# Two scatters of token rows and three groups of transposing fetches, moved behind the recurrent loop

## The chip, the core and the metric

The kernel runs on one core of a Trainium2 chip. The core has five engines with queues of their own: PE (TensorE, matrix products; its weight loads are shown apart as PEld), DVE (VectorE), ACT (ScalarE), POOL (GpSimd) and SP (SyncE, which here only issues transfers). Transfers run on 16 DMA engines that all queues share. The metric is device time of one launch in microseconds (us), the median of several runs; lower is better.

## What is computed

Three stages follow each other: a gated linear recurrence over 768 positions for 4 x 8 heads, a layer of 8 experts of which each of the 3072 tokens takes its best two, and a dense layer with a tanh-like nonlinearity.

```python
# recurrence, t = 0..767
state = f[:, :, t, :, None] * state + np.einsum('bhd,bhe->bhde', k[:, :, t], v[:, :, t])
y[:, :, t] = np.einsum('bhd,bhde->bhe', q[:, :, t], state)
...
logits = x @ w_gate
noisy_logits = logits + log1p(exp(x @ w_noise)) * noise
top2 = argpartition(-noisy_logits, 2, axis=1)[:, :2]                # two experts for each token
for e in range(8):
    h = maximum(x[mask] @ w1[e], 0.0)
    out[mask] += top2_w[mask, k, None] * (h @ w2[e])
...
h = x @ w_in
g = h - tanh(h)
return g @ w_out
```

## The kernel before, in words

**The recurrent loop.** The 768 positions of 4 batches are cut into 24 blocks of 128, and a loop `for j in range(NT)` (NT = 24) takes one block in each iteration: scaled keys and queries (`scaled`, POOL's product at L468), scores (`scores`, L484), a mask on DVE (L490), outputs (`outputs`, L499 and L507), states, and the rows of x (`x_rows`, `x_split`). Iterations are counted from 0 in the code, so the 22nd and 23rd are j = 21 and j = 22.

**Routing and scatters.** Four blocks make a group. Three iterations after a group's last block, `place` works out the row in the table `xs` for each of its tokens and both of its experts. That makes 8 scatters for a group (4 blocks x 2 experts), 48 in all; here they are numbered 0 to 47. A scatter is an indirect DMA of 128 rows that POOL issues in `post` (L652). `post` is called twice in an iteration: once early, right behind the POOL product, and once behind `states`. The second call may be paced: POOL first copies one element of a result (`pace`, L327), so that it waits for that result. Early calls put a memset in front (L650) if the instruction before was a scatter as well. Behind the loop one scatter is posted in each step of the expert layer, paced by that step's activated tile `hs`. Table rows above 640 of each expert are cleared by 8 transfers (`clear`, L409) in the iterations j = 20 to 22.

**The expert layer.** `moe_steps` lists (expert, block, f): 8 steps f for each expert and block, the blocks in the order (0,0), (1,0), (2,0), (0,1), (1,1), and so on. Step n computes the first product of its own entry (`first_products`, L218, 9 matmuls that read all columns of the tile `xt`) and the second product of the entry two steps back (`second_products`, L237). Steps 0 to 2 lie in the loop's last iterations, 3 and 4 right behind it, the others in the loop over n. So n = 8 is the first step of (1,0), n = 16 that of (2,0), n = 24 that of (0,1).

**Fetches of expert parts.** `load_x(e, blk, pieces)` fills `xt` with transposing transfers from `xs` (L188), 128 rows to a piece, issued by SP. A fetch must come behind the scatters that can write its rows. For three blocks the code bounds those: `EARLY` says that (1,0) needs the blocks j < 16, that is scatters 0 to 31, and (2,0) needs j < 20, scatters 0 to 39. A later block, (0,1) too, needs all 48.

**What sets the order.** The schedule is written by hand: each engine runs its instructions in the order of the program. SP is one such queue: a fetch that waits for a scatter holds up all behind it, the expert weights (`load_weights`, L149, through a ring of 4 buffers, split on ACT and DVE at L158 and L159), the stores of results (L274) and the fetches of later weights (`decode_load`, L783).

Of the kernel before, what the change touches and what calls it, by code (L numbers as in the profile page):

```python
# [21 lines left out]
B, H, S, D = 4, 8, 768, 48  # L22
N, DM, NE, FF, F2 = 3072, 384, 8, 1024, 2048
NCH = S // 128
NT = B * NCH
# [5 lines left out]
def blocks(e):  # L31
    cut = {0: 320, 1: 384, NE - 1: 384}.get(e, 512)
    return (0, cut), (cut, CAP - cut)
# [3 lines left out]
EARLY = {(0, 0): 12, (1, 0): 16, (2, 0): 20}  # L37
# [40 lines left out]
def fast(ctx, tc, flag, f_cols, kq_cols, v_rows, gates, blank, void, w12, w_in, w_out, out):  # L78
# [96 lines left out]
    scatters = []  # L175
    xtp = ctx.enter_context(tc.tile_pool(name="xtp", bufs=3))

    def new_xt(key):
        XT[key] = xtp.tile([128, 6, 512], F16, name="xt")

    def load_x(e, blk, pieces):
        if pieces.start == 0:
            new_xt((e, blk))
        at, n = blocks(e)[blk]
        lo, hi = pieces.start * 128, min(n, pieces.stop * 128)
        if lo >= hi:
            return
        t = nc.sync.dma_start_transpose(XT[e, blk][:, :, lo:hi], xs[e * CAP + at + lo:e * CAP + at + hi, :])  # L188
        if (e, blk) in EARLY:
            early_rows[e, blk].append(t)  # L190
            for o in scatters[:2 * EARLY[e, blk]]:
                tc.add_manual_dep(t.ins, o.ins.name, mybir.DependencyInfo(mybir.DependencyClass.Sync, mybir.DependencyReason.DATA),
                                  reason="rows of earlier tokens")
            for o in scatters[2 * EARLY[e, blk]:]:
                tc.declare_no_dep(t.ins, o.ins, reason="slots of late tokens are clamped to later rows")
# [130 lines left out]
    def pace(t):  # L326
        nc.gpsimd.tensor_copy(spacer, t)  # L327
# [27 lines left out]
    with ExitStack() as actx:  # L355
# [3 lines left out]
        T = {}  # L359
# [199 lines left out]
        groups = [[4 * g + i for i in range(4)] for g in range(NT // 4)]  # L559
        ends = {js[-1] for js in groups}  # L560
        group_of = {j: g for g, js in enumerate(groups) for j in js}
# [82 lines left out]
        def post(n, behind=None):  # L644
            while n and posts:
                r, j = posts.pop(0)
                if behind is not None:
                    pace(behind)
                elif near[0]:
                    nc.gpsimd.memset(spacer, 0.0)  # L650
                near[0] = True
                sc = nc.gpsimd.indirect_dma_start(  # L652
                    out=xs, out_offset=bass.IndirectOffsetOnAxis(ap=yslot[:, j, r:r + 1], axis=0),
                    in_=T["x16", j], in_offset=None)
                for o in scatters:
                    tc.declare_no_dep(sc.ins, o.ins, reason="slots of other tokens")
                for o in clears if j < CLEARED else ():
                    tc.declare_no_dep(sc.ins, o.ins, reason="these tokens' slots lie below the cleared rows")
                for key, first in EARLY.items():
                    for o in early_rows[key] if j >= first else ():  # L660
                        tc.declare_no_dep(sc.ins, o.ins, reason="slots of late tokens are clamped to later rows")
                scatters.append(sc)
                n -= 1

        chains, posts = [], []
        LOGITS, ROWS, PLACES = ({js[-1] + i: g for g, js in enumerate(groups)} for i in (1, 2, 3))
# [36 lines left out]
        for j in range(NT):  # L703
            if j == NT - 4:
                load_v(NT - 1)
            else:
                load_all(j + 3)
            if j == NT - 5:
                load_kq(NT - 1)
                load_x(0, 0, range(3))  # L710
            for e in {NT - 4: (0, 1, 2), NT - 3: (3, 4, 5), NT - 2: (6, 7)}.get(j, ()):
                clear(e)
            if j == NT - 1:
                load_x(1, 0, range(1))
            scores(j + 1)
            carried(j)
            scaled(j + 2)
            post(1)
            decays(j + 2)
            mask(j + 1)  # L720
            copies = [step(at[j]) for step, at in ((group_logits, LOGITS), (group_rows, ROWS)) if j in at]
            for c in copies:
                next(c)
            if j in PLACES:
                advance(100)
                chains.append(place(PLACES[j]))
                advance(1)
            decay(j + 3)
            logs(j + 3)
            sums(j + 3)  # L730
            for c in copies:
                next(c, None)
            outputs(j)
            advance(2)
            states(j)
            post(j > min(PLACES), None if j // B < NCH - 1 else T["yT", group_of[j]][0:1, j - groups[group_of[j]][0], 0, 0:1])
            if j >= NT - 3:
                moe_first(*moe_steps[j - NT + 3])
            key_rows(j + 1)
            advance(2)  # L740
            if j:
                x_rows(j - 1)
                x_split(j - 1)
            weights(j)
            advance(2)
# [2 lines left out]
        tags.update(ph=cycle(("b3", "b6", "b4", "b7")))  # L748
        moe_first(*moe_steps[3])
        post(1, corner(((0, 0), 3)))  # L750
        load_x(1, 0, range(1, 2))
        last = len(groups) - 1
        for _ in group_logits(last):
            pass
# [9 lines left out]
        advance(100)  # L764
        moe_products(4)
        post(1, corner(((0, 0), 4)))
        load_x(1, 0, range(2, 3))

    gath = ctx.enter_context(tc.tile_pool(name="gath", bufs=4))
    win = ctx.enter_context(tc.tile_pool(name="win", bufs=1))  # L770
# [126 lines left out]
    for n in range(4, len(moe_steps) + LAG):  # L897
        if n > 4:
            moe_products(n)
        if n == 5:  # L900
            chains.append(place(last, "b3"))
            advance(100)
        if n >= len(moe_steps):
            put_results()
            continue
        e, blk, f = moe_steps[n]
        nxt = order[n // 8 + 1] if n // 8 + 1 < len(order) else None
        if n > 4:
            post(1, corner(((e, blk), f)))
        if n == 12:  # L910
            rows_of = count_rows()
        if n == 14:
            take_rows(rows_of)
        if 9 <= n < 13:
            assert len(scatters) >= 2 * EARLY[2, 0]
            load_x(2, 0, range(n - 9, n - 8))
        for _ in range(2 if n < 6 else 1):
            if ahead:
                split_weights(*ahead.pop(0))
                if coming:  # L920
                    load_weights(*coming.pop(0))
        if n == 20:
            nc.sync.dma_start(y_rows[(NE - 2) * CAP + 512:(NE - 1) * CAP, :], void)
        if n == 17:
            assert not posts
            nc.vector.tensor_tensor(dv, top2[:, :, 1], top2[:, :, 0], op=OP.subtract)
            nc.scalar.activation(wt[:, 1, :], dv, AF.Exp)
            nc.vector.tensor_scalar(wt[:, 0, :], wt[:, 1, :], 1.0, 1e-9, op0=OP.add, op1=OP.add)
            nc.vector.reciprocal(wt[:, 0, :], wt[:, 0, :])
            nc.vector.tensor_scalar(wt[:, 0, :], wt[:, 0, :], SM / (SX * SW * SW), None, op0=OP.mult)  # L930
            nc.vector.tensor_tensor(wt[:, 1, :], wt[:, 1, :], wt[:, 0, :], op=OP.mult)
        if nxt and 17 <= n < 21 or n >= 24 and f < 4 and nxt:
            assert not posts
            load_x(*nxt, range((n - 1) % 8, (n - 1) % 8 + 1) if n < 24 else range(f, f + 1))
        m = n - len(moe_steps) + 16
        if 3 <= m < 11:
            gather_y((m - 3) // 2, (m - 3) % 2, corner(((e, blk), f)))
        if m == 7:
            new_xt(("m", 0))
        if m in (6, 9, 11, 13):  # L940
            combine((m - 6) // 2)
        if m in (7, 10, 12, 14):
            put_m((m - 7) // 2)
        if e >= 2 and blk == (e in (2, NE - 1)):
            if f < 5:
                load_weights(e + 1, f + 3)
            split_weights(e + 1, f)
        if f >= 5:
            if 0 < e < NE - 2 and blk == 1:
                load_weights(e + 2, f - 5)  # L950
            if e == NE - 1 and blk == 0:
                load_weights(NE, f - 5)
        if e < NE - 1:
            for i in range(2) if e < 2 else (blk,):
                if blk or e >= 2:
                    weight_sum(e, f, i)
        for _ in range((2 if f == 2 else 1) if f in (2, 4, 6) else 0):
            if DEC:
                decode_put(*DEC.pop(0))
        if n > 12 and f % 2 and todo:  # L960
            if loads_ahead:
                decode_load(*loads_ahead.pop(0))
            decode_work(*todo.pop(0))
        if 9 < n < 13:
            decode_load(*loads_ahead.pop(0))
        put_results()
# [83 lines left out]
    for n in range(M + FF_LAG):  # L1050
        if n < M:
            blk, f = steps[n]
# [315 lines left out]
```

## Time and profile before

| what | value |
|---|---|
| median of 3 runs | 892.25 us (891.9 to 892.9) |
| the profiled execution | 893.01 us, span 891.2 us |
| PE busy | 879.7 us, 99% of the span |
| ACT, DVE, POOL busy | 67%, 64%, 20% |
| chain that ended last | PE 95%, POOL 1%, ACT 1%, DMA 1%, "issue" 1% |
| mean granted TensorE clock | 0.996 of full speed |
| DMA: SP's queue / POOL's queue | 40.5% / 7.1% of 16 engines' span |

How to read it: the span is what the profiler saw of the program on the core, and the execution's own time is a little longer. PE is busy nearly all the time, so a wait of PE makes the launch longer by its whole length, and work of another engine counts only where PE waits for it. The loop ends near 123 us; the steps n = 5 to n = 24 lie between 127 and 190 us.

### The profile page before, as it was taken

What the parts mean: (1) busy time and instruction counts of PE and PEld (TensorE: products, weight loads), DVE (VectorE), ACT (ScalarE), POOL (GpSimd) and SP (SyncE); (2) the same over time, 40 slices, a digit from 0 to 9 for tenths busy, and PEclk for the clock granted to TensorE, in tenths of its full rate; (3) what the DMA queues carried; (4) which work ended last, traced back from release to release, by engine and by line L of the source; (5) the groups of instructions that cost most, each with busy time, mean ns of one, the idle gap of its engine ahead of it and who ended that gap; (6) DMA issues with size and microseconds to landing.
All of it is one profiled execution on the core that took longest, in us unless ns stands there. A gap on an engine that the chain in (4) does not pass through costs nothing.

```text
span 891.2 us, 17622 instructions
## 1 busy us (share of the span) xinstructions
PE 879.7 (99%) x6380; PEld 528.4 (59%) x6380; DVE 574.7 (64%) x1167; ACT 599.8 (67%) x1561; POOL 175.5 (20%) x240
## 2 busy tenths in 40 slices
PE   9999999999999999999999999999999999999996
PEld 8888766555665656556566555555555555555553
DVE  8988965733486565667657766565565665665664
ACT  8989755656786566668658776666666567557653
POOL 3588835100000000000004050140230320410000
PEclk9999999999999999999999999999999999999999
DMA  9899898844595575739356523041230220320101
GB/s 271 199 260 285 271 296 253 274 104 82 163 245 172 145 216 110 213 105 240 105 152 170 148 67 44 19 101 24 61 74 10 72 63 10 90 53 1 37 1 40
DMA packets 112335, 116.86 MB, mean 131 GB/s; under 512 B 68208, under 2 KB 91376, under 8 KB 112080
## 3 DMA queue, kind: packets, MB, share of 16 engines
q1 hardware_dynamic: 105792, 96.11, 40.5%
q0 software_dynamic: 6144, 18.88, 7.1%
q8 instruction: 69, 1.13, 0.5%
q14 instruction: 42, 0.34, 0.1%
q10 hardware_dynamic: 288, 0.39, 0.1%
HBM read 72.88 MB, written 30.38 MB: 116 GB/s over the span
## 4 chain that ended last, share of the span: by engine, by line
PE 95%; POOL 1%; ACT 1%; issue 1%; DMA 1%; DVE 0%; SPq 0%; POOLq 0%
PE py L237 43%; PE ph L218 43%; PE pA L484 2%; PE pY L507 2%; PE pY L499 1%; PE warm L671 1%; DMA kq<-in_kq_cols 1%; PE pkr L523 1%; PE pX L550 1%; POOL kqT L468 1%; POOL xs L652 1%; PE pK L536 0%; PE pt L570 0%; ACT eneg L463 0%; ACT yT L513 0%
## 5 line engine op out<-in xcount | busy, mean ns | idle before, releaser
L237 PE MATMUL py<-wsplit,hs 128*128 128x384 f16 x2384 | 423.3, 326 | 0.0
L237 PEld LDWEIGHTS <-hs 128*128 128x128 f16 x2384 | 233.2, 98 | 164.8
L218 PE MATMUL ph<-xt,wsplit 128*128 128x512 f16 (+7 forms) x1152 | 213.2, 330 | 0.0
L218 PE MATMUL ph<-xt,winS 128*128 128x512 f16 x864 | 201.6, 379 | 0.0
L218 PEld LDWEIGHTS <-wsplit 128*128 128x128 f16 x1152 | 112.6, 98 | 78.2 <-issue 0.9
L862 DVE SCALAR_TENSOR_TENSOR s<-s,z 128x512 f32<-128x512 f32 x96 | 66.4, 692 | 137.2 <-ACT s L859 137.2
L858 ACT ACTIVATE z<-ph 128x512 f32<-128x512 f32 x96 | 57.3, 597 | 127.5 <-PE ph L218 127.5
L218 PEld LDWEIGHTS <-winS 128*128 128x128 f16 x864 | 84.5, 98 | 91.9
L252 DVE SCALAR_TENSOR_TENSOR hs<-ph,hs 128x256 f16<-128x256 f32 (+2 forms) x192 | 79.5, 442 | 80.9 <-ACT hs L244 80.2
L244 ACT ACTIVATE hs<-ph 128x512 f16<-128x512 f32 (+3 forms) x128 | 65.6, 513 | 81.0 <-PE ph L218 71.2
L159 DVE SCALAR_TENSOR_TENSOR wsplit<-raw,wsplit 128x768 f16<-128x768 f32 x72 | 68.6, 955 | 17.6 <-ACT wsplit L158 16.5
L164 ACT ACTIVATE junk<-wsplit 128x384 f16<-128x384 f16 x144 | 74.2, 515 | 1.4
L859 ACT ACTIVATE s<-z,bias_a 128x512 f32<-128x512 f32 x96 | 69.3, 722 | 3.1
L327 POOL CAST spacer<-hs 1x1 f32<-1x1 f16 x22 | 5.7, 258 | 329.1 <-ACT hs L244 328.5
L864 DVE SCALAR_TENSOR_TENSOR g<-s,ph 128x512 f32<-128x512 f32 x96 | 66.0, 687 | 6.1
L871 DVE TENSOR_TENSOR hs<-g,hs 128x512 f16<-128x512 f32 x96 | 65.7, 685 | 0.1
L158 ACT ACTIVATE wsplit<-raw 128x768 f16<-128x768 f32 x72 | 60.0, 834 | 3.9 <-DMA raw<-in_w 3.4
L327 POOL COPY spacer<-g 1x1 f32<-1x1 f32 x40 | 20.0, 500 | 215.9 <-DVE g L864 199.7
L870 ACT ACTIVATE hs<-g 128x512 f16<-128x512 f32 x96 | 58.8, 613 | 1.1 <-DVE g L864 1.1
L829 POOL DMA_INDIRECT g<-y_rows,yslot x48 | 52.8, 1099 | 19.6 <-issue 10.6
L652 POOL DMA_INDIRECT xs<-xkeep,yslot x48 | 49.7, 1035 | 15.9 <-issue 10.1
L266 ACT ACTIVATE yo<-py 128x384 f32<-128x384 f32 x26 | 12.7, 490 | 36.8 <-PE py L237 36.8
(149 smaller groups left out, 855.9 us busy)
## 6 DMA issues: line engine op xcount, KB each, us to landing
raw<-in_w SPq DMA_DIRECT2D x64, 384.0 KB
y_rows<-yo SPq DMA_DIRECT2D x48, 192.0 KB
kq<-in_kq_cols SPq DMA_DIRECT2D x42, 192.0 KB
w<-in_moe_w_out SPq DMA_DIRECT2D x32, 192.0 KB
w<-in_moe_w_in SPq DMA_DIRECT2D x24, 256.0 KB
v<-in_v_rows SPq DMA_DIRECT2D x24, 192.0 KB
out<-o SPq DMA_DIRECT2D x22, 192.0 KB
f<-in_f_cols SPq DMA_DIRECT2D x40, 96.0 KB
```

Source lines behind the costliest of these rows:

```text
L158: nc.scalar.activation(t[:, 0], raw, AF.Copy, scale=SW)
L159: nc.vector.scalar_tensor_tensor(t[:, 1], raw, SW, t[:, 0], op0=OP.mult, op1=OP.subtract)
L164: nc.scalar.activation(junk[:, :DM], RING[e, f][:, 0, 3 * i:3 * i + 3, :].rearrange("p a b -> p (a b)"), AF.Square, accum_out=wsum[:, 8 * ...
L218: nc.tensor.matmul(ph[:, :n], l, x[:, r, :n], start=(o == 0), stop=(o == 8))
L237: nc.tensor.matmul(p[:max(m, 128)], l, r, start=(f == 0 and o == 0), stop=(f == last and o == len(ops) - 1))
L244: nc.scalar.activation(hs[:, :n], ph[:, :n], AF.Relu, accum_out=hacc[:, at:at + 1])
L252: nc.vector.scalar_tensor_tensor(hs[:, at:at + hi - lo], ph[:, lo:hi], 0.0, hs[:, lo:hi], op0=OP.max, op1=OP.subtract)
L859: nc.scalar.activation(s, z, AF.Square, scale=1.0 / SZ, bias=bias_a)
L862: nc.vector.scalar_tensor_tensor(s, s, ZD, z, op0=OP.add, op1=OP.mult)
L864: nc.vector.scalar_tensor_tensor(g, s, 0.5, ph, op0=OP.mult, op1=OP.mult)
L870: nc.scalar.activation(hs[:, :512], g, AF.Copy)
L871: nc.vector.tensor_tensor(hs[:, 512:], g, hs[:, :512], op=OP.subtract)
```

## The change

The second `post` of the iterations j = 21 and j = 22 posts nothing any more. The scatters behind them move up by two places: the loop ends with scatter 31 in place of 33, and the last one, 47, is posted at n = 18 in place of n = 16. So that each fetch still stands behind the scatters that it needs, the fetches move too:

- (1,0): its three pieces were issued at j = 23, behind step 3 and behind step 4; now behind step 3, behind step 4 and at n = 5.
- (2,0): its four pieces were issued at n = 9 to 12, now at n = 11 to 14.
- (0,1): its four pieces were issued at n = 17 to 20, now at n = 19 to 22; the six small instructions that make the weights `wt` of the two experts move from n = 17 to n = 19.

```diff
@@ -181,6 +181,7 @@
     def load_x(e, blk, pieces):
         if pieces.start == 0:
             new_xt((e, blk))
+        assert (e, blk) not in EARLY or len(scatters) >= 2 * EARLY[e, blk], (e, blk, len(scatters))
@@ -710,8 +711,6 @@
-            if j == NT - 1:
-                load_x(1, 0, range(1))
             scores(j + 1)
@@ -733,7 +732,7 @@
             states(j)
-            post(j > min(PLACES), None if j // B < NCH - 1 else T["yT", group_of[j]][0:1, j - groups[group_of[j]][0], 0, 0:1])
+            post(j > min(PLACES) and j not in (NT - 3, NT - 2), None if j // B < NCH - 1 else T["yT", group_of[j]][0:1, j - groups[group_of[j]][0], 0, 0:1])
@@ -748,7 +747,7 @@
         post(1, corner(((0, 0), 3)))
-        load_x(1, 0, range(1, 2))
+        load_x(1, 0, range(1))
@@ -764,7 +763,7 @@
         post(1, corner(((0, 0), 4)))
-        load_x(1, 0, range(2, 3))
+        load_x(1, 0, range(1, 2))
@@ -911,9 +910,11 @@
-        if 9 <= n < 13:
+        if n == 5:
+            load_x(1, 0, range(2, 3))
+        if 11 <= n < 15:
             assert len(scatters) >= 2 * EARLY[2, 0]
-            load_x(2, 0, range(n - 9, n - 8))
+            load_x(2, 0, range(n - 11, n - 10))
@@ -921,7 +922,7 @@
-        if n == 17:
+        if n == 19:
             assert not posts
             nc.vector.tensor_tensor(dv, top2[:, :, 1], top2[:, :, 0], op=OP.subtract)
@@ -929,9 +930,9 @@
-        if nxt and 17 <= n < 21 or n >= 24 and f < 4 and nxt:
+        if nxt and 19 <= n < 23 or n >= 24 and f < 4 and nxt:
             assert not posts
-            load_x(*nxt, range((n - 1) % 8, (n - 1) % 8 + 1) if n < 24 else range(f, f + 1))
+            load_x(*nxt, range(n - 19, n - 18) if n < 24 else range(f, f + 1))
```

**POOL's queue at the end of the loop, before**, from the last product for the loop (L468) on. L652 is a scatter out of a group's rows (`xkeep0`: group 3, `xkeep1`: group 4), L474 a copy of decays, L327 the pacing copy, L650 the memset:

```order
L468 TENSOR_TENSOR kqT_2072<-eneg_2069,kq2_152 128x512
L652 DMA xs_61<-xkeep0_174,yslot_96 6656x768
L474 COPY gall_95<-eneg_2069 128x4
L327 COPY spacer_94<-yT_2033 1x1
L652 DMA xs_61<-xkeep0_174,yslot_96 6656x768
L650 MEMSET spacer_94 1x1
L652 DMA xs_61<-xkeep0_174,yslot_96 6656x768
L327 COPY spacer_94<-yT_2033 1x1
L652 DMA xs_61<-xkeep0_174,yslot_96 6656x768
L650 MEMSET spacer_94 1x1
L652 DMA xs_61<-xkeep1_175,yslot_96 6656x768
```

The same place now (line numbers are one higher):

```order
L469 TENSOR_TENSOR kqT_2072<-eneg_2069,kq2_152 128x512
L653 DMA xs_61<-xkeep0_174,yslot_96 6656x768
L475 COPY gall_95<-eneg_2069 128x4
L653 DMA xs_61<-xkeep0_174,yslot_96 6656x768
L651 MEMSET spacer_94 1x1
L653 DMA xs_61<-xkeep0_174,yslot_96 6656x768
L328 COPY spacer_94<-yT_2033 1x1
L653 DMA xs_61<-xkeep0_174,yslot_96 6656x768
L328 CAST spacer_94<-hs_2267 1x1
L653 DMA xs_61<-xkeep1_175,yslot_96 6656x768
```

Behind the copy of decays two scatters still follow each other with no wait for another engine's result; the third of that row, scatter 31, now belongs to j = 23. The first scatter of group 4 has moved behind the loop and waits for an `hs` tile first.

**SP's queue around the fetch of (2,0), before** (`xt_2572` is the tile of (2,0); `raw` are expert weights, `w64` later weights, `y_rows` results; DMASW in the brackets are the scatters' semaphores):

```order
L188 DMA_TRANSPOSE xt_2572<-xs_61 128x6x128 [waits DMASW5_49,DMASW4_49,DMASW6_49,DMASW3_49,DMASW7_49,DMASW2_49,DMAHW6_49,DMASW1_49,DMASW0_49]
L149 DMA raw_2577<-in_w12 128x768 [waits DMAHW2_49,DVE_49]
L274 DMA y_rows_62<-yo_2560 128x384 [waits Activation_49,Pool_49]
L274 DMA y_rows_62<-yo_2562 128x384 [waits DVE_49]
L274 DMA y_rows_62<-yo_2564 64x384 [waits DVE_49]
L188 DMA_TRANSPOSE xt_2572<-xs_61 128x6x128 [waits DMAHW3_49]
L149 DMA raw_2613<-in_w12 128x768 [waits DMAHW4_49,DVE_49]
L783 DMA w64_2615<-in_moe2_w_out 128x192 [waits DMAHW5_49,PE_49,Pool_49]
L188 DMA_TRANSPOSE xt_2572<-xs_61 128x6x128 [waits DMAHW6_49]
L149 DMA raw_2646<-in_w12 128x768 [waits DMAHW7_49,DVE_49]
L783 DMA w64_2648<-in_moe2_w_out 128x192 [waits DMAHW0_49]
L188 DMA_TRANSPOSE xt_2572<-xs_61 128x6x128 [waits DMAHW1_49]
```

The same fetch now (its tile is `xt_2634`):

```order
L275 DMA y_rows_62<-yo_2559 64x384 [waits DVE_49]
L149 DMA raw_2605<-in_w12 128x768 [waits DMAHW3_49,DVE_49]
L782 DMA w64_2607<-in_moe2_w_out 128x192 [waits PE_49,Pool_49]
L189 DMA_TRANSPOSE xt_2634<-xs_61 128x6x128 [waits DMASW5_49,DMASW4_49,DMASW6_49,DMASW3_49,DMASW7_49,DMASW2_49,DMAHW4_49,DMASW1_49,DMASW0_49]
L149 DMA raw_2639<-in_w12 128x768 [waits DMAHW5_49,DVE_49]
L782 DMA w64_2641<-in_moe2_w_out 128x192 [waits DMAHW6_49]
L189 DMA_TRANSPOSE xt_2634<-xs_61 128x6x128 [waits DMAHW7_49]
L149 DMA raw_2680<-in_w12 128x768 [waits DMAHW0_49,DVE_49]
L782 DMA w64_2682<-in_moe2_w_out 128x192 [waits DMAHW1_49]
L189 DMA_TRANSPOSE xt_2634<-xs_61 128x6x128 [waits DMAHW2_49]
L149 DMA raw_2713<-in_w12 128x768 [waits DMAHW3_49,DVE_49]
L782 DMA w64_2715<-in_moe2_w_out 128x192 [waits DMAHW4_49]
```

The stores of results and two weight loads now stand ahead of the first piece; between two pieces there is always one load of expert weights and one of later weights. The fourth piece is the next row behind those shown.

## Rows read from the trace of the kernel before

**Rows 1.** The page, part 1: busy time of each engine.

```profile
PE 879.7 (99%) x6380; PEld 528.4 (59%) x6380; DVE 574.7 (64%) x1167; ACT 599.8 (67%) x1561; POOL 175.5 (20%) x240
```

**Rows 2.** Chain that ended last, 85 to 175 us: start, duration, what.

```profile
109.95 0.54 issue
...
111.02 1.18 issue
...
113.49 2.51 PE ph L218 x9
...
118.22 1.33 PE ph L218 x9
```

**Rows 3.** Windows of 2 us: length, five engines' busy time, clock, DMA share, GB/s.

```profile
110.00:112.00 2.00, 0.53 (x3) 0.28 (x3) 1.18 (x3) 0.00 (x0) 0.98 (x2) 1.00 1.03 417
112.00:114.00 2.00, 1.80 (x17) 1.20 (x17) 1.11 (x4) 0.47 (x1) 0.00 (x0) 0.71 1.00 417
114.00:116.00 2.00, 2.00 (x9) 1.27 (x8) 0.00 (x0) 0.13 (x1) 1.22 (x3) 0.50 0.97 390
```

**Rows 4.** Timeline of POOL, the scatters: start, duration, what, idle before.

```profile
108.92 0.99 POOL L652 DMA_INDIRECT xs<-xkeep,yslot  x1 [0.16 <-issue]
...
110.22 0.97 POOL L652 DMA_INDIRECT xs<-xkeep,yslot  x1 [0.21 <-issue]
...
114.95 0.97 POOL L652 DMA_INDIRECT xs<-xkeep,yslot  x1 [0.52 <-DMA xs<-in_blank]
...
122.47 0.98 POOL L652 DMA_INDIRECT xs<-xkeep,yslot  x1 [0.16 <-ACT junk L247]
...
139.00 1.75 POOL L652 DMA_INDIRECT xs<-xkeep,yslot  x1 [0.51 <-issue]
...
145.95 0.98 POOL L652 DMA_INDIRECT xs<-xkeep,yslot  x1 [0.16 <-issue]
...
162.81 0.98 POOL L652 DMA_INDIRECT xs<-xkeep,yslot  x1 [0.51 <-issue]
```

**Rows 5.** Timeline of PE: start, duration, what.

```profile
135.88 1.63 PE L218 MATMUL ph<-xt,wsplit 128*128 128x384 f16 x9
...
159.11 2.10 PE L218 MATMUL ph<-xt,wsplit 128*128 128x512 f16 x9
...
162.51 2.10 PE L218 MATMUL ph<-xt,wsplit 128*128 128x512 f16 x9
...
189.27 1.87 PE L218 MATMUL ph<-xt,wsplit 128*128 128x448 f16 x9
```

**Rows 6.** Timeline of SP's queue: start and time of issuing.

```profile
126.14 1.21 SPq L188 DMA_TRANSPOSE xt<-xs  x1
...
129.70 0.33 SPq L149 DMA_DIRECT2D raw<-in_w  x1
...
142.74 1.95 SPq L188 DMA_TRANSPOSE xt<-xs  x1
...
145.41 1.44 SPq L274 DMA_DIRECT2D y_rows<-yo  x3
...
151.46 0.42 SPq L783 DMA_DIRECT2D w<-in_moe_w_out  x1
151.94 2.15 SPq L188 DMA_TRANSPOSE xt<-xs  x1
...
167.82 1.21 SPq L188 DMA_TRANSPOSE xt<-xs  x1
...
176.19 1.30 SPq L188 DMA_TRANSPOSE xt<-xs  x1
```

**Rows 7.** DMA packets in three windows: 145 to 145.5, 157 to 157.5, 157.5 to 158.

```profile
DMA packets 274, 0.06 MB, mean 124 GB/s; under 512 B 274, under 2 KB 274, under 8 KB 274
...
DMA packets 325, 0.21 MB, mean 420 GB/s; under 512 B 294, under 2 KB 294, under 8 KB 325
...
DMA packets 79, 0.20 MB, mean 390 GB/s; under 512 B 16, under 2 KB 16, under 8 KB 79
```

## The prediction, as it went on record

> **What bounds the kernel now.** I read the page first. PE is busy for 879.7 us of a span of 891.2 [rows 1], so whatever the other engines do counts only where PE stops. So next the chain of waits: it shows where PE stops, and it has long pieces of PE alone from 113 us to the end. The only stop near the change is in iteration j = 22: two pieces called "issue", 0.54 and 1.18 us, in which PE waits for nothing that the profile shows [rows 2]. The windows show what follows: PE works 0.53 us out of the 2 us from 110 on, and then the granted clock is 0.71 and 0.50 of full speed for two windows, the lower of the chip's two levels (1.2 instead of 2.4 GHz) for much of that time [rows 3]. The same nine matmuls that take 1.33 us at full clock take 2.51 there [rows 2]. Then I looked at where PE will need the fetched tiles, in PE's timeline: n = 8 starts at 135.88, n = 16 at 159.11, n = 24 at 189.27 [rows 5]. SP's timeline says when the pieces are issued [rows 6], and the packet counts when they land: a piece moves in packets under 512 bytes, and nothing else here does so in such number [rows 7].
>
> About 0.2% (1.8 us) is what a measurement of this kernel can tell from no change.
>
> **The change part by part.** The sum is made against the profiled execution's own 893.01 us; the median of the runs is 892.25, 0.76 lower.
>
> *The two scatters out of j = 21 and j = 22.* By name the change takes a scatter (0.99 us of POOL) out of each. But POOL's last product for the loop stands ahead of both, so nothing that PE waits for gets earlier. And the order shows what takes their place: the scatters of the next early calls move up. Before, scatters 29 and 30 started at 108.92 and 110.22 and scatter 31 at 114.95 [rows 4]. Now 29 and 30 still follow directly behind the same copy, so until 114.95 POOL and the DMA queues carry the same load, and PE's stop at 110 to 112 lies before that. I take 0 for it. Only scatter 31 leaves that stretch, 128 rows of 1536 bytes or 0.2 MB out of a stream of about 400 GB/s [rows 3], 0.5 us of DMA time that PE does not wait for. The ends are a gain of 3.1 us, if the stop goes with its slow clock (a rival below), and a loss of 0.5.
>
> *The pieces of (1,0), needed at n = 8.* SP no longer stops for scatter 31 inside j = 23. What is late next is scatter 31 itself, posted in the second place of j = 23, which before started at 122.47 [rows 4]. The third piece used to be issued at 126.14; it now stands behind the load that was issued at 129.70 [rows 6], so it starts near 130.05. With the slowest landing that the trace has (5.56 us, below) it is there at 135.6, and n = 8 starts at 135.88: 0.3 us to spare. I take 0, at most 1 us.
>
> *The pieces of (2,0), needed at n = 16.* This is the term. All nine matmuls of n = 16 read all four pieces.
> - The first piece waits for scatter 39. Before, this scatter started at 139.00, took POOL 1.75, and SP issued the piece at 142.74, 1.99 us behind its end [rows 4, 6]. Now scatter 39 takes the place that 41 had, in step n = 10: start 145.95, 0.98 us [rows 4]. The first piece is then issued at 145.95 + 0.98 + 1.99 = 148.92, 6.2 us later than before.
> - From the first piece's issue to the fourth's it was 151.94 - 142.74 = 9.20 us [rows 6]. SP was issuing without a pause, so what stands between counts: the three stores (1.44) are now ahead of the first piece, and one more load of later weights (0.42) stands between. 9.20 - 1.44 + 0.42 = 8.18, so the fourth piece is issued at 157.10.
> - How long a piece takes to land: the fourth, issued at 151.94, has its last large batch of small packets (294) before 157.5, and 16 in the next window: 5.56 us [rows 6, 7]. The first, issued at 142.74 into empty queues, is done by 145.5: 2.76 us [rows 6, 7]. Those are the two ends: 159.86 and 162.66. The nearer case is the slow one, since weight loads, later weights and scatters are queued between the pieces as before. I take off what the stores' 480 KB (by their shapes) cost there (1.2 us at 390 to 420 GB/s [rows 3, 7]) and add 0.5 for the additional load of 192 KB: 4.86 us, landing at 161.96.
> - PE would start n = 16 at 159.11. It stops for 161.96 - 159.11 = 2.85 us; the ends are 0.75 and 3.55. Nothing covers this: the second product of the same step stands behind the first in PE's queue.
> - The slow clock after it: the stop in j = 22 was shorter (0.54 + 1.18 us and little work between), and the clock fell behind it. The clock that was missing is 0.29 x 2 + 0.50 x 2 = 1.58 us [rows 3]; the nine matmuls alone lost 1.18 [rows 2]. I take 1.4; the ends are 0, if dense work ahead of the stop keeps the clock up, and 1.6.
>
> *The pieces of (0,1), needed at n = 24.* They wait for scatter 47, which moves by two steps of 162.51 - 159.11 = 3.40 us [rows 5], from 162.81 [rows 4] to 169.6. The first piece was issued 5.01 us behind that scatter's start, the fourth 8.37 behind the first [rows 6]: 174.6 and 183.0. With the slow landing it is there at 188.6, before 189.27; if PE stops at n = 16, both sides shift alike. 0, at most 1 us. The small instructions for `wt` move with SP's and DVE's slack; PE does not read them here. 0.
>
> The sum: 2.8 + 1.4 = 4.2 us. 893.01 + 4.2 = 897.2 for a profiled execution, and 896.4 as a median. The ends of the terms give +0.7 and +5.1, that is 892.9 to 897.4.
>
> **The rivals.**
>
> *A: the fourth piece of (2,0) is late* (above): 896.4.
>
> *B: it is in time.* SP no longer stands still before 142.74, so the loads and stores behind that wait go out earlier and the queues may be empty when the pieces come. Then a piece lands as the first one did, in 2.76 us, and everything turns on whether the fourth is issued before 159.11 - 2.76 = 156.35; I have 157.10. For it: 0.75 us is little, and the lost time of scatter 39 (1.75 before) may come back on POOL. Against it: SP needs some 8 us for the row of issues however empty the queues are, and between two pieces more transfers are queued than the DMA engines carry in that time. It gives 892.25, give or take 0.5. The Trainium skill ("DMA: Bandwidth & Descriptors", section "Anatomy of one DMA — SWDGE (gpsimd) path") speaks for it: it fits a fixed 2.0 us and the bytes at 436 GB/s, by which I estimate 2.45 us for a piece of 197 KB, a landing at 159.55 and a stop of only 0.4 us. The trace agrees for the first piece (2.76) and differs by a factor of two for the fourth (5.56), where other transfers are ahead of it.
>
> *C: faster, because PE's stop in j = 22 goes.* All engines are quiet from 110 to 112 while the DMA share is 1.03 and 1.00 [rows 3]; if traffic is what starves them, less of it helps. It would give back 0.54 + 1.18 and the 1.4 of slow clock, 3.1 us: 889.1, if the fourth piece is in time as well. It decides from the moment that scatter 29 or 30 starts later than now. Against it: by the order they do not.
>
> *D: a second tile is late too*, at n = 8 or n = 24, where I have 0.3 and 0.7 us to spare: about 1.5 us and once more 1.4 for the clock, on top of A: 899.3.
>
> **How the numbers follow.** A has 0.66, B 0.18, C 0.06, D 0.10. A is slower by more than 0.2% unless both its stop is near its lower end and the clock stays up: 0.58 slower, 0.08 within. B lies within 0.2% but for 0.01 that is faster. So faster 0.07, within 0.2% 0.25, slower 0.68. The predicted time is A's. The range 892.0 to 898.4 takes in A and most of B and leaves out C, a little of B below and the upper part of D.
>
> **What would show each step.** In the profile after: scatters 29 and 30 start within 0.5 us of 108.8 and 110, and the chain still has its "issue" and its slow clock at 110 to 116 (else C). The first piece of (2,0) is issued near 148.9 and the fourth near 157.1. PE's first matmuls of n = 16 have idle time before them, released by the fetch into `xt`, some 2.8 us long, and the next windows have a granted clock under 1. n = 8 and n = 24 start with no idle time. From n = 16 on, all of PE's work is later by one and the same amount. The prediction is wrong if PE goes through n = 16 without a stop, or if it stops where I have none.

## The result, and the profile after

The changed kernel takes 897.3 us (median of 6 runs, 896.28 to 899.16), the kernel before 892.58 in the same rounds (6 runs, 891.6 to 894.53). The ratio is 1.0053, with a 95% interval of 1.0037 to 1.0068: slower by 4.7 us. The prediction said 896.4, in a range of 892.0 to 898.4, and gave "slower" 0.68. The profiled execution took 897.11 us with a span of 895.3, against 893.01 and 891.2 before.

The page's part 1 after, which answers to [rows 1]:

```profile
span 895.3 us, 17624 instructions
...
PE 879.6 (98%) x6380; PEld 527.0 (59%) x6380; DVE 575.3 (64%) x1167; ACT 598.9 (67%) x1561; POOL 175.6 (20%) x239
```

PE has as many instructions and as much work as before; the span is 4.1 us longer. So PE stands still for longer. The waits of PE, summed over the whole span (line waited for, total us, times, longest), say where:

```profile
PE ph L219 <- issue: 3.6, 2, 3.3
```

One stop of 3.3 us, in front of a `ph` matmul. PE's timeline from n = 15 to n = 17 (start, duration, what, idle before it), to be held against [rows 5]:

```profile
155.11 1.63 PE L219 MATMUL ph<-xt,wsplit 128*128 128x384 f16 x9
156.57 1.63 PE L238 MATMUL py<-wsplit,hs 128*128 128x384 f16 x9
161.49 3.54 PE L219 MATMUL ph<-xt,wsplit 128*128 128x512 f16 x9 [3.30 <-issue]
164.83 1.92 PE L238 MATMUL py<-wsplit,hs 128*128 128x384 f16 x9
166.58 2.11 PE L219 MATMUL ph<-xt,wsplit 128*128 128x512 f16 x9
...
134.81 1.63 PE L219 MATMUL ph<-xt,wsplit 128*128 128x384 f16 x9
...
193.34 1.87 PE L219 MATMUL ph<-xt,wsplit 128*128 128x448 f16 x9
```

The third row is n = 16. PE was through with n = 15 and would have started at 156.57 + 1.63 = 158.20; it starts at 161.49. Then its nine matmuls take 3.54 us in place of 2.10, and the nine of the second product 1.92 in place of 1.63. The last two rows, n = 8 (with n = 7 ahead of it) and n = 24, have no idle time. The view names no releaser ("issue"). SP's queue (start, time of issuing) and the packets (windows 160 to 160.5, 160.5 to 161, 161 to 161.5) name it:

```profile
148.45 1.23 SPq L189 DMA_TRANSPOSE xt<-xs  x1
149.77 0.52 SPq L149 DMA_DIRECT2D raw<-in_w  x1
150.35 0.42 SPq L782 DMA_DIRECT2D w<-in_moe_w_out  x1
150.83 1.22 SPq L189 DMA_TRANSPOSE xt<-xs  x1
...
153.24 1.34 SPq L189 DMA_TRANSPOSE xt<-xs  x1
...
155.72 1.21 SPq L189 DMA_TRANSPOSE xt<-xs  x1
```

```profile
DMA packets 520, 0.14 MB, mean 276 GB/s; under 512 B 518, under 2 KB 518, under 8 KB 520
...
DMA packets 244, 0.18 MB, mean 362 GB/s; under 512 B 199, under 2 KB 199, under 8 KB 244
...
DMA packets 51, 0.16 MB, mean 313 GB/s; under 512 B 0, under 2 KB 0, under 8 KB 51
```

The small packets of the fetch end before 161; half a microsecond later PE runs. The fourth piece was issued at 155.72, so its packets are through after 5.3 us and PE starts after 5.77.

The windows of 2 us (length, busy time of PE, PEld, DVE, ACT and POOL, granted clock, DMA share, GB/s), at the end of the loop, which answers to [rows 3], and at the stop:

```profile
110.00:112.00 2.00, 1.04 (x28) 0.72 (x21) 1.58 (x4) 0.01 (x1) 1.78 (x3) 1.00 1.11 455
112.00:114.00 2.00, 1.69 (x19) 1.09 (x19) 1.77 (x4) 0.17 (x1) 0.26 (x1) 1.00 1.11 445
114.00:116.00 2.00, 2.00 (x29) 1.48 (x26) 0.21 (x1) 1.27 (x5) 0.00 (x0) 1.00 0.84 336
...
158.00:160.00 2.00, 0.20 (x2) 0.00 (x0) 1.30 (x3) 0.90 (x2) 0.98 (x1) 1.00 1.01 352
160.00:162.00 2.00, 0.51 (x3) 0.30 (x4) 0.91 (x3) 0.00 (x0) 0.00 (x0) 1.00 1.13 321
162.00:164.00 2.00, 2.00 (x7) 0.63 (x6) 0.00 (x0) 0.00 (x0) 0.00 (x0) 0.50 1.05 413
164.00:166.00 2.00, 2.00 (x9) 0.93 (x8) 0.16 (x1) 0.88 (x3) 0.06 (x1) 0.65 0.79 299
```

Behind the stop the granted clock is 0.50 and 0.65: the lower of the two levels, 1.2 GHz, for all of one window and most of the next. At the end of the loop PE still stops, but in this execution the clock stays at 1.00 there, where it had fallen to 0.71 and 0.50 before.

The balance, up to the start of n = 17 (166.58 against 162.51 [rows 5], 4.07 later): n = 16 was due 0.91 earlier than before (158.20 against 159.11); the stop adds 3.30, the first product's slow clock 1.44, the second's 0.29. That is 4.12, 0.05 more than the 4.07 because a product starts a little before the one ahead of it ends; the span is 4.1 longer. Nothing behind n = 17 adds to it: n = 24 is 4.07 later too (193.34 against 189.27 [rows 5]).

### The profile page after: what moved, and what is told of

Its sections match the earlier page's. It is cut to its first block, busy times and chain, and to the rows that moved or that the text cites. A ratio compares the mean times of both kernels' runs of the same rounds, so it can differ in the third digit from the quotient of the medians.

```text
span 895.3 us, 17624 instructions
## 1 busy us (share of the span) xinstructions
PE 879.6 (98%) x6380; PEld 527.0 (59%) x6380; DVE 575.3 (64%) x1167; ACT 598.9 (67%) x1561; POOL 175.6 (20%) x239
## 4 chain that ended last, share of the span: by engine, by line
PE 88%; POOL 6%; issue 2%; ACT 2%; DVE 1%; DMA 1%; POOLq 0%; DVEq 0%
PE py L238 43%; PE ph L219 42%; POOL xs L653 3%; POOL kqT L469 2%; PE pY L508 1%; POOL st L545 1%; DMA w<-in_moe_w_out 1%; PE pA L485 1%; POOL gall L475 0%; PE pY L500 0%; DMA f<-in_f_cols 0%; PE pkr L524 0%; ACT eneg L464 0%; PE pX L551 0%; ACT krows L526 0%
## 5 line engine op out<-in xcount | busy, mean ns | idle before, releaser
L653 POOL DMA_INDIRECT xs<-xkeep,yslot x48 | 51.6, 1075 | 12.6 <-issue 11.4
```

What stands on the lines that cost most here:

```text
L653: sc = nc.gpsimd.indirect_dma_start(out=xs, out_offset=bass.IndirectOffsetOnAxis(ap=yslot[:, j, r:r + 1], axis=0), in_=T["x16", j], in_off ...
```

## The experiments

The theory: the whole loss is the fourth piece of (2,0), late at n = 16, with the slow clock behind the stop. The rivals: that the scatters moved behind the loop, or the later fetch of (0,1), cost something themselves; and that the eight clears at the end of the loop feed PE's stop in j = 22. The first four share one set of runs of the kernel before (median 892.17 of 29), the last three another (892.39 of 28).

**The fetches back in their places, with the scatters of the changed kernel.** Two scatters each at n = 5 and 6 make up for the two that were left out (the comments in this diff and the next are added here, and lines are cut at `...`):

```diff
-            post(1, corner(((e, blk), f)))
+            post(2 if n < 7 else 1, corner(((e, blk), f)))
-        if 11 <= n < 15:
+        if 9 <= n < 13:                  # the pieces of (2,0)
-        if nxt and 19 <= n < 23 or ...
+        if nxt and 17 <= n < 21 or ...   # the pieces of (0,1), wt at 17
```

> The changed kernel, but two scatters are posted in each of the steps n = 5 and n = 6, so that scatter 39 is back at n = 8; the fetches of (2,0) and (0,1) stand at n = 9 to 12 and n = 17 to 20 again. The loop's end and the fetch of (1,0) stay as changed. Theory (the fourth piece of (2,0) is late, because scatter 39 gates the first): no stop at n = 16, some 5 us less than the changed kernel, 892 us or a little under, since the loop's end was 0.9 us shorter in the changed kernel's trace. Rival (moving scatters from the loop to the expert steps costs time by itself, by more DMA traffic there): between 894 and 897, with waits spread over n = 5 to 16.

Measured: 892.28 us, ratio to before 1.0008 [0.9996, 1.0021]. PE's timeline at n = 8 and at n = 16:

```profile
135.08 1.62 PE L219 MATMUL ph<-xt,wsplit 128*128 128x384 f16 x9 [0.33 <-DMA xt<-xs]
...
158.79 2.10 PE L219 MATMUL ph<-xt,wsplit 128*128 128x512 f16 x9 [0.33 <-DMA xt<-xs]
160.73 1.63 PE L238 MATMUL py<-wsplit,hs 128*128 128x384 f16 x9
```

The loss is gone although the loop's scatters are those of the changed kernel, and what is left of the stop at n = 16, 0.33 us, is now put down to the fetch into `xt`: PE starts 6.85 us behind the fourth piece's issue (151.94). The scatters outside the loop cost nothing that can be told from noise; the later fetches do. At n = 8, PE waits 0.33 us for the pieces of (1,0), which are fetched as in the changed kernel.

**The later fetches alone, with the scatters of the kernel before.**

```diff
-        if 9 <= n < 13:
+        if 11 <= n < 15:                 # the pieces of (2,0)
-        if nxt and 17 <= n < 21 or ...
+        if nxt and 19 <= n < 23 or ...   # the pieces of (0,1), wt at 19
```

> The kernel before with its scatters as they were, but the fetches of (2,0) and (0,1) two steps later in SP's program, as in the change. Theory (it is the scatter that the first piece waits for, not the place in the program): scatter 39 has landed long before, SP runs ahead of the steps, the first piece is issued near 145.3 and the fourth near 152.6, PE does not stop at n = 16: 892 to 893. Rival (the later place alone makes the fourth piece late): a stop of 2 to 3.5 us at n = 16 and 895 to 897.

Measured: 892.3 us, 1.0007 [0.9995, 1.0018]. PE's timeline:

```profile
157.36 2.10 PE L218 MATMUL ph<-xt,wsplit 128*128 128x512 f16 x9 [1.25 <-DMA w<-in_moe_w_out]
159.30 1.63 PE L237 MATMUL py<-wsplit,hs 128*128 128x384 f16 x9
```

I had expected no stop. There is one of 1.25 us: the first piece is issued at 143.28 and the fourth at 151.23, and PE starts 6.13 us behind that. PE itself is 3 us earlier here than in the kernel before (n = 15 starts at 153.03 against 156.18), so what counts is how far the fourth issue is ahead of n = 15: 1.80 us, against 4.24 before [rows 6]. In the kernel before with its clears spread (the last experiments), where n = 15 is early as well (154.47), it is 3.99 and there is no stop. So the later place in the program is enough for a stop, and the scatter that comes later makes it longer. The clock stays up behind 1.25 us. In the median the stop doesn't show, but the interval (up to 1.6 us) doesn't exclude it, and this profile has hardly a stop in j = 22 (PE is busy 1.71 of the 2 us from 110 on, at a clock of 1.00).

**The changed kernel with the four pieces of (2,0) back to back.**

```diff
-        if 11 <= n < 15:
+        if n == 11:
-            load_x(2, 0, range(n - 11, n - 10))
+            for i in range(4):
+                load_x(2, 0, range(i, i + 1))
```

> The changed kernel, but all four pieces of (2,0) are issued one behind the other at n = 11, with no weight loads between. The scatters stay as changed, so the first piece is still issued near 148.5. Theory (beside the gate, the two loads between each pair of pieces make the fourth late): the fourth is issued near 152.4 and lands by 157, no stop at n = 16, 892 us. Rival (the transposing fetches are slow by themselves and queue behind each other): the fourth lands after 159, a stop of 1 us or more, 894 or above.

Measured: 891.67 us, 0.9995 [0.9984, 1.0006]. SP's queue, then PE's timeline:

```profile
148.37 5.27 SPq L189 DMA_TRANSPOSE xt<-xs  x4
153.74 0.52 SPq L149 DMA_DIRECT2D raw<-in_w  x1
154.31 0.44 SPq L782 DMA_DIRECT2D w<-in_moe_w_out  x1
```

```profile
156.26 1.63 PE L238 MATMUL py<-wsplit,hs 128*128 128x384 f16 x9
157.73 2.10 PE L219 MATMUL ph<-xt,wsplit 128*128 128x512 f16 x9
```

The first piece waits for the same late scatter as in the changed kernel (148.37 against 148.45), yet n = 16 starts with no idle time: the fourth piece is issued some 3 us earlier, and no load is queued ahead of it. This also answers what the `w` in the stop of the run before is: the loads of later weights now go out behind the pieces, later than in the changed kernel, and PE doesn't wait for them. With one edit the whole loss is gone, so everything else that the change moves ((1,0), (0,1), `wt`, the two scatters) costs nothing that can be measured. It is the fastest version that was run, but it can't be told from the kernel before.

**The stop filled with work.** The changed kernel with 50 matmuls of 128 columns ahead of n = 16's first product, so that PE works while it waits:

```diff
+                if (e, blk, f) == (2, 0, 0):
+                    for _ in range(50):
+                        nc.tensor.matmul(ph[:, :128], ones, ones, start=True, stop=True)
```

> The changed kernel with 50 matmuls of 128 columns on a constant tile in front of the first product of n = 16, into the same bank, some 2.8 us at full clock, so that PE works while it waits; their sums are overwritten. Theory (of the 5 us, 3.3 are the stop and 1.7 the slow clock behind it): the first real matmul of n = 16 still starts near 161.5, the granted clock stays 1.00, the nine matmuls take 2.1 instead of 3.5 us: 1.5 to 1.8 us less than the changed kernel, near 895.6. Rival (the nine matmuls are slow for another reason, such as reading a tile that is still being written): no gain, 897.3 or more.

Measured: 895.73 us, 1.0037 [1.0023, 1.0051], 1.6 us less than the changed kernel's median (1.4 by the two ratios). PE's timeline and its windows:

```profile
156.27 1.63 PE L219 MATMUL ph<-xt,wsplit 128*128 128x384 f16 x9
...
159.20 2.96 PE L297 MATMUL ph<-ones 128*128 128x128 bf16 x50
163.09 2.10 PE L219 MATMUL ph<-xt,wsplit 128*128 128x512 f16 x9 [0.94 <-issue]
165.03 1.63 PE L238 MATMUL py<-wsplit,hs 128*128 128x384 f16 x9
```

```profile
160.00:162.00 2.00, 2.00 (x39) 1.98 (x36) 1.83 (x5) 0.07 (x1) 0.36 (x1) 1.00 1.15 272
162.00:164.00 2.00, 1.06 (x8) 0.46 (x6) 0.21 (x1) 0.00 (x0) 0.00 (x0) 1.00 1.12 355
...
110.00:112.00 2.00, 0.81 (x17) 0.44 (x9) 1.32 (x3) 0.00 (x0) 0.97 (x1) 1.00 0.92 383
112.00:114.00 2.00, 1.94 (x24) 1.51 (x25) 1.77 (x4) 0.60 (x1) 0.00 (x0) 0.87 1.11 451
114.00:116.00 2.00, 2.00 (x10) 1.39 (x9) 0.00 (x0) 0.30 (x1) 0.00 (x0) 0.50 0.95 390
```

n = 16 comes no earlier (6.82 us behind n = 15's start, 6.38 in the changed kernel), but at full clock: 2.10 and 1.63. So the two parts of the loss are apart: 1.73 us in the rows (3.54 and 1.92 in the changed kernel) are the clock, the rest is the wait. The medians agree (1.6 us) but don't show it by themselves, since the intervals of the two ratios overlap. The last three rows are from the end of the loop of the same execution: there the clock did fall this time, with the same instructions as in the changed kernel, so this execution (897.15 us) is no faster than the changed kernel's profile. Its mean granted clock is 0.996; four of the six executions have 0.997 to 0.999, while all six of the changed kernel have 0.995 or 0.996.

**Half of the change.** One scatter fewer (in j = 22 alone), the fetches one step later:

```diff
-            post(j > min(PLACES) and j not in (NT - 3, NT - 2), ...
+            post(j > min(PLACES) and j != NT - 2, ...
-        if 11 <= n < 15:
+        if 10 <= n < 14:
-        if nxt and 19 <= n < 23 or ...
+        if nxt and 18 <= n < 22 or ...
```

> Half of the change: only j = 22 posts one scatter fewer, so the last scatters move by one place; the fetches of (2,0) and (0,1) move by one step (n = 10 to 13 and n = 18 to 21), that of (1,0) as in the change. Theory (the fourth piece follows scatter 39, one step of some 2.9 us for each place; the changed kernel's stop was 3.3 us, the time to spare before about 1.5): the fourth piece comes some 2.9 us earlier than in the changed kernel, the stop at n = 16 is 0.3 to 0.6 us and too short for the clock to fall: 892 to 893. Rival (the stop does not follow the scatter's place, but comes from the queues being full at that time): a stop of 1.5 us or more, 894 to 896.

Measured: 894.54 us, 1.0023 [1.0005, 1.0041]. SP's queue, then PE's timeline:

```profile
146.02 1.22 SPq L189 DMA_TRANSPOSE xt<-xs  x1
...
153.21 2.00 SPq L189 DMA_TRANSPOSE xt<-xs  x1
```

```profile
159.31 2.10 PE L219 MATMUL ph<-xt,wsplit 128*128 128x512 f16 x9 [1.25 <-DMA w<-in_moe_w_out]
161.25 1.63 PE L238 MATMUL py<-wsplit,hs 128*128 128x384 f16 x9
```

The pieces go out 2.4 to 2.5 us earlier and the stop is 2.05 us shorter, without the slow clock in this execution: the stop falls with the lateness, as the theory wants. The stop is larger than I had expected (1.25 us): PE starts 6.10 us behind the fourth piece's issue. My figure for the landing was too short again. The median is above the theory's 892 to 893, in the rival's range, though the stop is not the 1.5 us that the rival wanted. The profiled execution (893.28 us, mean granted clock 0.999) is among the faster of the eleven; four have 0.992 to 0.995 and take 894.02 to 900.75 us. So this version loses its clock in some executions; where, no trace shows.

**The eight clears spread over j = 15 to 22**, in the kernel before and in the version with the pieces back to back:

```diff
-            for e in {NT - 4: (0, 1, 2), NT - 3: (3, 4, 5), NT - 2: (6, 7)}.get(j, ()):
+            for e in range(max(0, j - NT + 9), j - NT + 10) if NT - 9 <= j < NT - 1 else ():
```

> The kernel before, its 8 clearing transfers spread over the iterations j = 15 to 22, one in each, in place of eight within j = 20 to 22. It asks where PE's stop with no named wait at 110 to 112 us comes from, which varies from run to run. Theory (that stop comes from the DMA queues being full of clearing transfers): PE goes through j = 22 without it and without the slow clock behind it in the profile, 889 to 891, and the runs lie closer together. Rival (it has another cause, or the spread transfers hold up the loads of earlier iterations by as much): 892 or more, with the idle time still there or moved to j = 15 to 20.

> The changed kernel with the four pieces of (2,0) issued together at n = 11 and the clearing transfers spread over j = 15 to 22. Theory (both stops have their own cause and add up): no stop at n = 16, none in j = 22, as fast as the kernel before with the spread alone or up to 0.5 us faster, 889 to 891. Rival (the spread gives nothing): 891.5 to 892.5, as with the pieces together alone.

Measured: 892.97, 1.0005 [0.9995, 1.0015], and 891.97, 0.9996 [0.9986, 1.0007]. Neither gains. Two windows of the first:

```profile
98.00:100.00 2.00, 1.57 (x32) 1.40 (x32) 2.00 (x4) 2.00 (x5) 1.76 (x4) 1.00 0.89 274
...
110.00:112.00 2.00, 1.54 (x31) 0.92 (x19) 1.82 (x4) 0.00 (x0) 1.78 (x3) 1.00 0.96 387
```

and the first of these two in the kernel before and in the changed kernel, whose clears are not spread either:

```profile
98.00:100.00 2.00, 2.00 (x50) 1.69 (x54) 1.94 (x5) 2.00 (x5) 1.99 (x3) 1.00 0.54 194
...
98.00:100.00 2.00, 1.49 (x30) 1.26 (x32) 2.00 (x4) 2.00 (x5) 1.82 (x3) 1.00 0.58 168
```

From 110 on PE is busy for 1.54 us where it was 0.53 [rows 3], but from 98 on it now lacks 0.43. That doesn't show that the idle time moved with the clears: without the spread the changed kernel lacks 0.51 from 98 on too, and the version with the later fetches alone is busy for 1.71 from 110 on. The idle time differs that much between executions. What decides is the time: the interval leaves room for a gain of 0.45 us at most, the theory wanted 1.4 or more. The theory that the traffic of the clears at the end of the loop costs the time fell.

## Why the prediction was right, step by step

**What bounds the kernel.** Right. PE's work is unchanged, and the time moved by PE's stop and clock alone.

**The two scatters out of the loop.** The value, 0, is right: the version with the pieces back to back has the same scatters and no loss. Scatters 29 and 30 kept their order but start at 109.59 and 110.88, not within 0.5 us of 108.8 and 110.0: the last iterations are some 0.7 us later than before as a whole, and POOL is late already at scatter 23 (96.22 against 95.46), ahead of all that the change moves. That the slow clock would stay at 110 to 116 was wrong for this execution: the stop stayed, the clock didn't fall. It fell in another kernel with the same instructions there (the one with the filler matmuls), so this differs between executions, and the profile of one doesn't settle it. It gave the changed kernel's profile 0.91 us at n = 16 that I hadn't counted on.

**(1,0) and (0,1).** Right: no idle time at n = 8 and n = 24. The two tiles that I had left 0.3 and 0.7 us to spare did not stop PE, so case D didn't come. At n = 8 it is close: with the same fetch, the version with the fetches back in their places waits 0.33 us there, and PE starts 6.30 us behind the third piece's issue (128.78), more than my slowest landing of 5.56.

**(2,0).** The mechanism is as forecast; the sizes, forecast and measured:

| term | forecast | measured |
|---|---|---|
| first piece issued | 148.92 | 148.45 |
| fourth piece issued | 157.10 | 155.72 |
| from its issue to PE's start | 4.86 us | 5.77 us |
| PE starts n = 16 | 161.96 | 161.49 |
| PE could have started | 159.11 | 158.20 |
| stop | 2.85 us | 3.30 us |
| slow clock | 1.4 us | 1.73 us |

Two errors offset each other. The row of issues takes 7.27 us from first to fourth, not 8.18: I had carried over the slow first issue of before (1.95 us [rows 6]), and now it takes 1.23. And the landing was mis-sized in the other direction: the last packets come 5.3 us behind the issue in place of 4.86, nearer to the slow end (5.56) than my allowance for the stores, and from there PE takes another half microsecond that I hadn't counted. In the five executions that stop at n = 16, all with a load of expert weights and one of later weights just ahead of the fourth piece, PE starts 5.77, 6.05, 6.10, 6.13 and 6.85 us behind the fourth issue. The stop follows how early that issue is: 4.24 us ahead of n = 15's start there is none (the kernel before), at 3.43 it is 0.33 (the fetches back), at 1.80 and 1.77 it is 1.25 (the later fetches alone, half of the change), and 0.61 behind it is 3.30 (the changed kernel).

So the near match of the profile, 897.11 against a forecast of 897.2, is luck: the stop and the slow clock, which went beyond my upper end of 1.6, cost 5.03 us where the sum had 4.2, and the 0.91 that n = 16 came earlier made up for it. The medians (4.7 us against 4.2) do not match as closely.

Case B would have come with pieces that land in 2.76 us. The Trainium skill ("DMA: Bandwidth & Descriptors", section "Anatomy of one DMA — SWDGE (gpsimd) path") has a fixed 2.0 us and the bytes at 436 GB/s, 2.45 us for such a piece by my estimate. That fit is for transfers that POOL issues, and SP issues the pieces, so the estimate carries it over to another path. The trace comes near it where nothing is queued ahead (2.76 us before [rows 6, 7]) and not for the fourth piece here, whose packets need 5.3 us. Back to back the fit is near again: in that version the fourth piece is issued at about 152.4, one issue of 1.2 us before the row's end, and its small packets (290) end before 155.5, some 3 us later:

```profile
DMA packets 305, 0.11 MB, mean 225 GB/s; under 512 B 290, under 2 KB 290, under 8 KB 305
...
DMA packets 29, 0.09 MB, mean 178 GB/s; under 512 B 0, under 2 KB 0, under 8 KB 29
```

These are its windows 155 to 155.5 and 155.5 to 156.

**The name of the wait.** I had said that the view would put the stop down to the fetch into `xt`. It says "issue" here, and in two experiments the load of later weights that is issued just ahead of the fourth piece. What shows that it is the fetch are the packets and the version with the pieces back to back, where the loads that stood between them go out behind them; in the version with the fetches back in their places the view names it.

**What stays open.** The medians differ by 4.7 us and the profiles by 4.1. The mean granted clock of every execution says how this can be. It is 0.996 in the three profiles with a slow clock at the end of the loop or at n = 16 (the kernel before, the changed one, the one with the filler matmuls), and 0.998 or 0.999 in the six others, where the clock is under 1.00 only behind 880 us. All six executions of the changed kernel have 0.995 or 0.996, but only 7 of 57 of the kernel before have 0.996 or less. So the profile of the kernel before, from which the sum started, is with its slow clock at the end of the loop not the usual case of that kernel. Where the clock fell in an execution that has no trace is not shown. Nor is it settled what PE's nameless stops at the end of the loop are. Loading of instructions is not what ends them in the kernel before: its instruction queues have packets in the windows 101 to 101.5 and 115.5 to 116, and none between (in the changed kernel 101.5 to 102 and 116.5 to 117).

## What to carry to other kernels

When a fetch is moved later, count from its last piece to the first use, and take the landing time from a piece with the same loads queued ahead of it, not from one in empty queues: here the last packets came 5.3 us behind the issue against 2.8, and PE started 5.8 to 6.9 us behind it. Here it also paid to issue pieces that are needed at once back to back, with what is needed later behind them; that alone took the whole loss back. And the stop of 3.3 us had a second price, the slow clock behind it, which could be measured apart by filling the stop with matmuls that nobody needs.

## What the runs showed of the hardware

- A stop of 1.25 us at n = 16 (the profiles of two kernels) left the granted clock at 1.00, one of 3.30 us was followed by 0.50 and 0.65. At the end of the loop, where PE is idle in pieces, the clock fell to 0.50 in two profiles (the kernel before and the one with filler matmuls) and stayed at 1.00 in the others, the changed kernel among them. PE's idle time from 110 to 114 us does not tell them apart: 1.67 and 1.25 us where it fell, 0.29 to 1.44 where it stayed.
- A transposing fetch of (2,0) took SP 1.2 to 1.3 us to issue in the changed kernel, and up to 2.15 before [rows 6]; in the half-way version the last of four took 2.00 again. A row of issues was not a sum of fixed prices.
